# Retention in steps of 64 tokens on quarters of the TensorE array, in a kernel of retention and a Mish feed-forward

## The chip, the core and the metric

The kernel runs on one core of one Trainium2 chip. The metric is the device time of one execution in microseconds; lower is better. Three runs of the kernel before gave 208.31, 208.77 and 209.69 us, a median of 208.77. One execution was taken with the hardware profiler: it took 209.11 us, and the span from its first to its last instruction is 207.2 us.

## The reference: what is computed

Retention over 4 sequences of 768 tokens with 8 heads of 64, then a feed-forward layer with the weights w_in (512 x 2048) and w_out (2048 x 512), in fp32 at its ends:

```
gamma = 1.0 - 2.0 ** (-5.0 - np.arange(H))
for t in range(S):
    state = gamma * state + k[t] (outer) v[t]      # 64x64 for each head
    y[t] = scale * q[t] @ state
x = y, as 3072 rows of 512
h = x @ w_in
g = h * np.tanh(np.log1p(np.exp(h)))               # Mish
out = g @ w_out
```

## The kernel before

**Chunks and blocks.** The 3072 tokens are 24 chunks of 128 (C, six in a sequence). Block 0 has the first four chunks, blocks 1 to 10 two each. (In all texts here blocks and chunks are counted from 0; the sixth block is block 5.) Each block goes through retention, a first product with w_in and Mish, and a second product with w_out.

**Retention of a chunk** is computed chunkwise, heads in four pairs. The decay within a chunk is in the scaled q and v that `casts` makes on POOL (L211 on), so no decay stands in the matmuls:
- `scores` (L258): at = k q, eight matmuls that contract over the 64 rows of a head, so a head takes half of the array's rows; two heads of a pair take the two halves.
- `mask` (L269): DVE multiplies at by a triangle and writes am in fp16.
- `outer` (L280): u_ps = k v for a pair of heads in one 128 x 128 matmul, four of them. Half of each result belongs to no head.
- `state` (L290): DVE adds the last state and multiplies by gcm, which holds the decay of 128 tokens and is zero off the heads' own blocks. The state is 128 x 512.
- `past` (L303): y_ps = state q, four matmuls over the whole array.
- `present` (L310): y_ps += v am, eight matmuls that write half of the columns each.
- ACT casts y_ps to xt (L392), the input of the first product.

`scores_two`, `outer_two` and `y_two` (L364 to L393) do this for the two chunks of a block, with PSUM tiles of the pool atps (two tiles of two banks each). The pool mmps has four tiles of one bank.

**The feed-forward of a block.** `g1` (L397) makes 128 x 512 of h_ps per step: eight matmuls of 256 columns for a block of two chunks, and Mish on ACT. Blocks 1 and 2 do the second product straight (`g2_mm`, L416, 128 x 512). From block 3 on (SEVEN = 3) `seven` (L478) does the second product as a 2 x 2 product of blocks with seven multiplications: DVE makes sums of g (sums_a, sums_b, sums_c: L464 to L476), TensorE does seven products of eight matmuls into the tiles pb, pe and px, ACT takes copies of a tile between them (`snap`, L502), and DVE writes the results (`done`, L507). A `snap` of pe must be over before pe is added to again.

**Order of the work.** The order is written out by hand. Each engine takes its instructions in the order in which the program names them. The loop at L657 runs the steps u of a block; `plan_of` (L638) says behind which step the work for the next block stands: outer_two behind u=0, scores_two behind u=3, and y_two (as a hook of `seven`, L525) after the third of the seven products. In blocks 1 and 2 scores, outer and y stand behind steps 7 to 14. `next_chunk` (L632) casts, transposes (q and k of a chunk by DMA on SP's queue) and issues loads that are three chunks ahead. Stores stand on SP's queue too (L170).

Of the kernel before, what the change touches and what calls it, by code (L numbers as in the profile page):

```python
# [16 lines left out]
def kernel(  # L17
# [45 lines left out]
    gp = ctx.enter_context(tc.tile_pool(name="rn_g", bufs=2))  # L63
    op = ctx.enter_context(tc.tile_pool(name="rn_o", bufs=5))
    mmps = ctx.enter_context(
        tc.tile_pool(name="rn_mmps", bufs=4, space=bass.MemoryType.PSUM))
    atps = ctx.enter_context(
        tc.tile_pool(name="rn_atps", bufs=2, space=bass.MemoryType.PSUM))

# [6 lines left out]
    ident = cpool.tile([P, P], FP16, name="ident")  # L76
    tri = cpool.tile([P, C], FP32, name="tri")
    gcm = cpool.tile([P, HP, P], FP32, name="gcm")
    warm = cpool.tile([P, 1], FP32, name="warm")
    nc.gpsimd.memset(ident, 0.0)  # L80
    nc.gpsimd.affine_select(  # L81
# [4 lines left out]
        out=tri, in_=tri, compare_op=ALU.is_gt, fill=1.0, base=0,  # L86
        pattern=[[-1, C]], channel_multiplier=1)

    tri_first = cpool.tile([P, CPB, C // CPB], FP32, name="tri_first")
    nc.gpsimd.memset(tri_first, 0.0)  # L90
    nc.gpsimd.affine_select(
        out=tri_first, in_=tri_first, compare_op=ALU.is_gt, fill=1.0, base=0,
        pattern=[[-1, CPB], [-CPB, C // CPB]], channel_multiplier=1)
    nc.vector.memset(warm, 0.0)
    nc.scalar.activation(warm, warm, AF.Mish)
    nc.vector.memset(gcm, 0.0)
# [5 lines left out]
    wout_ap = moe_w_out.rearrange("(fb p) c -> p fb c", p=P)  # L102

    qfirst_t = cpool.tile([P, HP, CPB, P], FP16, name="qfirst_t")
    loaded, cast, qkts, ats, ams, states, us, ys = {}, {}, {}, {}, {}, {}, {}, {}
    xts, gts, wins, wouts, wtmps = {}, {}, {}, {}, {}
    gtiles, tmats, gsums = {}, [], []
    SEVEN = 3
# [102 lines left out]
    def casts(g):  # L211
        qf, kf, vf = loaded.pop(g)
        qk16 = castp.tile([P, 2, H, D], FP16, name="qk16")
        q16, k16 = qk16[:, 0], qk16[:, 1]
        v16 = castp.tile([P, H, D], FP16, name="v16")
        if qf is not None:
            nc.gpsimd.tensor_tensor(  # L217
                q16, qf, qs.unsqueeze(2).broadcast_to((P, H, D)), op=ALU.mult)
        if g < CPB + 2:
            nc.scalar.mul(k16, kf, BOOST)  # L220
        else:
            nc.gpsimd.tensor_scalar(k16, kf, BOOST, None, op0=ALU.mult)  # L222
        nc.gpsimd.tensor_tensor(  # L223
            v16, vf, vs.unsqueeze(2).broadcast_to((P, H, D)), op=ALU.mult)
        cast[g] = (q16, k16, v16, qk16)

    def turn_by_dma(g):
        qkt = qktp.tile([P, H, C], FP16, name="qkt", bufs=4)
        nc.sync.dma_start_transpose(qkt, cast[g][3].rearrange("p a h d -> p (a h d)"))
        qkts[g] = (qkt[:, :HP], qkt[:, HP:])  # L230

# [15 lines left out]
    def turn(g):  # L247
        q16, k16 = cast[g][:2]
        t_ps = atps.tile([P, H, C], FP16, name="t_ps", tag="at")
        for i in range(HP):  # L250
            nc.tensor.transpose(t_ps[:, i], q16[:, 2 * i:2 * i + 2], ident)
        for i in range(HP):
            nc.tensor.transpose(t_ps[:, HP + i], k16[:, 2 * i:2 * i + 2], ident)
        qkt = qktp.tile([P, H, C], FP16, name="qkt", bufs=4)
        nc.vector.tensor_copy(qkt, t_ps)
        qkts[g] = (qkt[:, :HP], qkt[:, HP:])

# [61 lines left out]
    def last_of_batch(g):  # L319
        return g % NCH == NCH - 1  # L320
# [2 lines left out]

    def outer_one(g):
        if not last_of_batch(g):
            outer(g, mmps.tile([P, HP, P], FP32, name="u_ps", tag="mm"), states.get(g - 1))

    def xt_first(g, pairs=slice(None)):
        n = C // CPB
# [31 lines left out]

    def scores_two(blk):  # L364
        a = first[blk]
        scores(a)
        scores(a + 1)
        mask(a)
        mask(a + 1)

    def outer_two(blk):
        a = first[blk]
        u_ps = atps.tile([P, 2, HP, P], FP32, name="u_ps", tag="at")
        for j in range(2):
            if not last_of_batch(a + j):
                outer(a + j, u_ps[:, j])
        for j in range(2):
            if not last_of_batch(a + j):
                state(a + j)

    def y_two(blk):
        a = first[blk]
        y_ps = atps.tile([P, HP, 2, C], FP32, name="y_ps", tag="at")
        inter = a % NCH > 0
        if inter:
            past(a, lambda i: y_ps[:, i, 0], lambda i: i % 2 == 0)
        past(a + 1, lambda i: y_ps[:, i, 1], lambda i: not inter and i % 2 == 0)
        for j in range(2):
            present(a + j, lambda i: y_ps[:, i, j], lambda i: False)
        xt = xtp.tile([P, HP, TB], FP16, name="xt")  # L390
        xts[blk] = xt
        nc.scalar.copy(  # L392
            xt[:, :, :2 * C], y_ps.rearrange("p i j c -> p i (j c)"))  # L393

    def g1(blk, u):  # L397
        nt = BLOCKS[blk] * C
        per = TB // nt
        h_ps = mmps.tile([P, per, nt], FP32, name="h_ps", tag="mm")  # L400
        for j in range(per):
            s, f = divmod(u * per + j, FPS)
            for bp in range(NBP):
                nc.tensor.matmul(  # L404
                    h_ps[:, j], wins[s][f // 2][:, bp, f % 2 * P:(f % 2 + 1) * P], xts[blk][:, bp, :nt],
                    start=(bp == 0), stop=(bp == NBP - 1))
        room = NFB * TB // (2 * nt)
        at0, lies = divmod(u * per, room)
        if lies == 0:
            gtiles[blk, at0] = gp.tile([P, room, nt], FP16, name="g", tag="g", bufs=4)  # L410
        gt = gtiles[blk, at0][:, lies:lies + per]
        nc.scalar.activation(gt, h_ps, AF.Mish, scale=inv_boost3)  # L412
        for j in range(per):
            gts[blk, u * per + j] = gt[:, j]
# [62 lines left out]

    def seven(blk, hooks, last):  # L478
        n, hf = NFB // 2, d_model // 2
        ps = [mmps.tile([P, hf], FP32, name="o_ps", tag="mm") for _ in range(3)]  # L480
        pb, pe, px = ps
        osb = [op.tile([P, d_model], FP32, name="osb", tag="osb") for _ in range(2)]

        def a(i, j):
# [5 lines left out]
        def s(i):  # L490
            return lambda f: gsums[blk % 2][:, i - 1, f]
# [30 lines left out]
        mm(px, s(2), t(2))  # L522
        u2 = snap(px)
        sums_c(blk)
        for fn, *args in hooks:  # L525
            fn(*args)
        mm(pe, s(1), t(1), True)
        m5 = snap(pe)
        mm(px, s(3), t(3))
        done(1, 1, px, m5)  # L530
# [31 lines left out]
    def first_block():  # L562
# [18 lines left out]
        for g in range(CPB):  # L581
            last = g == CPB - 1
            if not last:
                cast_to(g + 2)
            scores(g)
            mask(g, 2 if last else 1)
            if g > 0:
                y_one(g - 1)
            if not last:
                at_tile(g + 1)  # L590
                outer_one(g)
                spin(g + 1, 2 if g else 8)
                turn_k(g + 1)
                state(g)
                spin(g + 1, (12, 10, 8)[g])
        y_one_in_halves(CPB - 1)
        outer_one(CPB - 1)
        cast_win(0)
# [16 lines left out]
        for u in range(2 * NFB):  # L615
            if u < NFB:
                g1(0, u)
            elif u < 2 * NFB - 2:
                w = u - NFB
                for t in range(CPB):  # L620
                    if w == 0:
                        o_tiles[t] = mmps.tile([P, d_model], FP32, name="o_ps", tag="mm")
                    g2_mm(o_tiles[t], 0, t, w)
            else:
                for t in range(CPB // 2) if u % 2 == 0 else range(CPB // 2, CPB):
                    for w in range(NFB - 2, NFB):
                        g2_mm(o_tiles[t], 0, t, w)
                    g2_out(o_tiles[t], 0, t, 1)
            for fn, *args in plan.get(u + 1, ()):
                fn(*args)  # L630

    def next_chunk(g):  # L632
        if g < NCK:
            cast_to(g + 1)
            turn_by_dma(g)
            load_to(g + 3)

    def plan_of(blk):  # L638
        a = first[blk] + 4
        if blk >= SEVEN:  # L640
            plan = {1: [(cast_to, a + 1), (next_chunk, a)],
                    7: [(cast_to, a + 2), (next_chunk, a + 1)]}
            if blk + 1 < len(BLOCKS):
                plan[0] = [(outer_two, blk + 1)]
                plan[3] = [(scores_two, blk + 1)]
            return plan
        early, then_seven = blk == 1, blk + 1 == SEVEN
        plan = {1: [(cast_to, a + 1)],
                (1 if early else 2 if then_seven else 4): [(cast_to, a + 1), (next_chunk, a)],
                (5 if early else 8): [(cast_to, a + 2), (next_chunk, a + 1)]}  # L650
        plan[10 if early else 7] = [(scores_two, blk + 1)]
        plan[12 if early else 10] = [(outer_two, blk + 1)]
        plan[14 if early else 13] = [(y_two, blk + 1)]
        return plan

    first_block()
    for blk in range(1, len(BLOCKS)):  # L657
# [20 lines left out]
            if extra:  # L678
                extra.pop(0)()
        if blk >= SEVEN:  # L680
            seven(blk, [] if last else [(y_two, blk + 1)], last)
    store_due(2 * NFB)


# [28 lines left out]
```

## Time and profile before

| What | us |
|---|---|
| median of three runs | 208.77 |
| the profiled execution | 209.11 |
| its span | 207.2 |
| TensorE (PE) busy | 199.7 |
| VectorE (DVE) busy | 118.6 |
| ScalarE (ACT) busy | 86.6 |
| GpSimd (POOL) busy | 77.1 |
| matmuls of 256 columns for h_ps (L404), 640 of them, each | 0.273 |
| the masks of blocks 1 to 10 (L275), each | 1.22 |
| a cast of y_ps to xt (L392), each | 1.01 |

PE is the matmuls, PEld the loads of the stationary operand, which lie beside them. A matmul's record is longer than the step to the next one, since matmuls are pipelined: starts of L404 are 0.109 us apart though each record is 0.273. Steps between starts therefore tell what a matmul costs in a row of them, and records do not. A line such as L404 is a line of the kernel as printed above. In the chain of waits each piece is followed back from the last instruction to what released it.

### The profile page before, as it was taken

How to read it: one execution, taken by the hardware profiler on the slowest of the kernel's cores; microseconds unless marked ns; L12 is line 12 of the kernel's file. 1: busy time of each engine (PE TensorE's matmuls, PEld its weight loads, DVE VectorE, ACT ScalarE, POOL GpSimd, SP SyncE). 2: the span in 40 equal slices, each digit the busy share in tenths (PEclk: the TensorE clock that was granted, in tenths of full speed). 3: DMA queues.
4: the chain of work that ended last, by engine and by line, in shares of the span. 5: the costliest groups of instructions: out<-in, count | busy, mean ns of one | idle time of the engine just before them, and what ended most of it. 6: DMA issues, size and time to landing. Idle time of an engine off the chain costs nothing.

```text
span 207.2 us, 4555 instructions
## 1 busy us (share of the span) xinstructions
PE 199.7 (96%) x1909; PEld 150.4 (73%) x1909; DVE 118.6 (57%) x184; ACT 86.6 (42%) x146; POOL 77.1 (37%) x72
## 2 busy tenths in 40 slices
PE   7798999999999999999999999999999999999993
PEld 2454444445865775788888888888888888898883
DVE  2696544257209779475666686474574773573062
ACT  2243665043540650464354363453453453453640
POOL 3242000326966186577547358267066000000000
PEclk9999999999999999999999999999999999999999
DMA  5999999998899999999999799696897910200202
GB/s 179 235 223 341 381 387 349 233 294 180 159 235 279 207 197 230 193 232 207 242 237 179 114 245 153 164 244 101 189 203 118 180 26 5 101 0 23 82 27 77
DMA packets 99989, 38.59 MB, mean 186 GB/s; under 512 B 90497, under 2 KB 94081, under 8 KB 99969
## 3 DMA queue, kind: packets, MB, share of 16 engines
q1 hardware_dynamic: 96704, 37.50, 85.6%
q10 hardware_dynamic: 3264, 0.81, 2.4%
q8 instruction: 15, 0.25, 0.5%
q14 instruction: 6, 0.04, 0.1%
HBM read 27.29 MB, written 6.29 MB: 162 GB/s over the span
## 4 chain that ended last, share of the span: by engine, by line
PE 80%; DMA 9%; SPq 7%; ACT 1%; DVE 1%; issue 1%; ACTq 0%
PE h_ps L404 38%; PE o_ps L498 24%; PE o_ps L418 9%; DMA wi<-in_moe_w_in_dram 5%; SPq L122 5%; DMA kf<-in_k_dram 3%; PE y_ps L315 3%; PE at L265 3%; PE y_ps L305 2%; PE u_ps L283 2%; SPq L140 1%; ACT xt L392 1%; SPq L181 0%; DVE win L157 0%; ACT qk L220 0%
## 5 line engine op out<-in xcount | busy, mean ns | idle before, releaser
L404 PE MATMUL h_ps<-xt,win 128*128 128x256 f16 (+1 forms) x704 | 88.0, 282 | 1.1 <-DVE win L157 0.7
L412 ACT ACTIVATE g<-h_ps 128x512 f16<-128x512 f32 x96 | 57.3, 597 | 58.3 <-PE h_ps L404 58.3
L404 PEld LDWEIGHTS <-win 128*128 128x128 f16 x704 | 67.9, 98 | 17.6 <-DVE win L157 1.6
L217 POOL TENSOR_TENSOR qk<-qf,qvs 128x512 f16<-128x512 f32 x20 | 22.3, 1117 | 61.4 <-DMA qf<-in_q_dram 54.0
L275 DVE TENSOR_TENSOR am<-at,tri 128x1024 f16<-128x1024 f32 x20 | 23.7, 1220 | 18.1 <-PE at L265 18.0
L223 POOL TENSOR_TENSOR v<-vf,qvs 128x512 f16<-128x512 f32 x24 | 25.7, 1072 | 17.4 <-DMA vf<-in_v_dram 11.4
L418 PE MATMUL o_ps<-wout,g 128*128 128x512 f16 x128 | 30.1, 380 | 0.0
L222 POOL TENSOR_SCALAR qk<-kf 128x512 f16<-128x512 f32 x18 | 27.5, 1528 | 4.1 <-DMA kf<-in_k_dram 2.9
L498 PEld LDWEIGHTS <-gsum 128*128 128x128 f16 x256 | 24.5, 98 | 3.4
L498 PE MATMUL o_ps<-tmat,gsum 128*128 128x256 f16 x192 | 23.5, 273 | 0.0
L418 PEld LDWEIGHTS <-g 128*128 128x128 f16 x128 | 11.7, 98 | 13.0 <-issue 0.3
L512 DVE TENSOR_TENSOR osb<-o_ps,snap 128x256 f32<-128x256 f32 x24 | 10.1, 422 | 19.0 <-ACT snap L504 15.9
L498 PEld LDWEIGHTS <-g 128*128 128x128 f16 x192 | 18.8, 98 | 2.2
L392 ACT CAST xt<-y_ps 128x1024 f16<-128x1024 f32 x10 | 10.1, 1012 | 21.6 <-PE y_ps L315 21.6
L467 DVE TENSOR_TENSOR gsum<-g 128x512 f16<-128x512 f16 x16 | 7.8, 490 | 13.3 <-ACT g L412 13.2
L498 PE MATMUL o_ps<-wout,g 128*128 128x256 f16 x128 | 15.3, 273 | 0.0
L504 ACT COPY snap<-o_ps 128x256 f32<-128x256 f32 x24 | 8.9, 373 | 13.7 <-PE o_ps L498 13.7
L298 DVE TENSOR_TENSOR su<-u_ps,st 128x512 f32<-128x512 f32 x13 | 9.0, 692 | 5.0 <-PE u_ps L283 4.8
L243 PE MATMUL at<-ident 128*128 128x512 f16 (+1 forms) x34 | 9.8, 411 | 1.3 <-POOL ident L81 1.3
L299 DVE TENSOR_TENSOR st<-su,gcm 128x512 f16<-128x512 f32 x13 | 9.1, 703 | 0.4
L220 ACT ACTIVATE qk<-kf 128x512 f16<-128x512 f32 x6 | 3.8, 630 | 12.8 <-DMA kf<-in_k_dram 12.8
L157 DVE CAST win<-wi 128x1024 f16<-128x1024 f32 x8 | 5.4, 692 | 6.1 <-DMA wi<-in_moe_w_in_dram 6.1
(59 smaller groups left out, 146.2 us busy)
## 6 DMA issues: line engine op xcount, KB each, us to landing
kf<-in_k_dram SPq DMA_DIRECT2D x23, 256.0 KB, 4.7
vf<-in_v_dram SPq DMA_DIRECT2D x23, 256.0 KB, 5.0
out_dram<-osb SPq DMA_DIRECT2D x22, 256.0 KB, 4.4
qf<-in_q_dram SPq DMA_DIRECT2D x19, 256.0 KB, 4.0
wt<-in_moe_w_out_dram SPq DMA_DIRECT2D x3, 1024.0 KB, 10.1
wi<-in_moe_w_in_dram SPq DMA_DIRECT2D x4, 512.0 KB, 7.6
wi<-in_moe_w_in_dram SPq DMA_DIRECT2D x2, 1024.0 KB, 11.1
qfirst<-in_q_dram SPq DMA_DIRECT2D x2, 512.0 KB, 5.0
```

Source lines behind the costliest of these rows:

```text
L122: queue.dma_start(loaded[g][n], (q, k, v)[n][b, :, c * C:(c + 1) * C].rearrange("h p d -> p h d"))
L217: nc.gpsimd.tensor_tensor(q16, qf, qs.unsqueeze(2).broadcast_to((P, H, D)), op=ALU.mult)
L222: nc.gpsimd.tensor_scalar(k16, kf, BOOST, None, op0=ALU.mult)
L223: nc.gpsimd.tensor_tensor(v16, vf, vs.unsqueeze(2).broadcast_to((P, H, D)), op=ALU.mult)
L243: nc.tensor.matmul(ats[g][:, 0, :m], ident, ident.unsqueeze(1).broadcast_to((P, m, P)), start=True, stop=True)
L275: nc.vector.tensor_tensor(am[:, :, i:i + n], at[:, :, i:i + n], keep.unsqueeze(1).unsqueeze(1).broadcast_to((P, 2, n, C)), op=ALU.mult)
L392: nc.scalar.copy(xt[:, :, :2 * C], y_ps.rearrange("p i j c -> p i (j c)"))
L404: nc.tensor.matmul(h_ps[:, j], wins[s][f // 2][:, bp, f % 2 * P:(f % 2 + 1) * P], xts[blk][:, bp, :nt], start=(bp == 0), stop=(bp == NBP - 1))
L412: nc.scalar.activation(gt, h_ps, AF.Mish, scale=inv_boost3)
L418: nc.tensor.matmul(o_ps, gts[blk, fb][:, t * P:(t + 1) * P], wouts[s][:, f, cols], start=(fb == 0), stop=(fb == NFB - 1))
L498: nc.tensor.matmul(o_ps, x(f), w(f), start=first and f == 0, stop=f == n - 1, skip_group_check=True)
L512: nc.vector.tensor_tensor(dst, o_ps, plus, op=ALU.add)
```

## The change

From block 2 on retention runs in steps of 64 tokens, so that every matmul of it is 64 x 64 with 64 columns and sits on a quarter of the array. The first half and the second half of a chunk have states of their own: `mid_of` makes the state at a chunk's middle, `state_of` that at its end, both compact (128 x 256, a head pair's two states below each other, no empty halves). The scores between the halves of a chunk are no longer computed; the state in the middle carries them. Only the diagonal 64 x 64 blocks of at are made and masked (`tri_half`).

`ready` gives outer products and scores as pairs of matmuls, `same` for the quarters on the array's diagonal and otherwise for the others; `run` takes from several streams in turn. `past_of` is on the diagonal quarters alone. Between `past_of` and `present_of`, which write the same banks from other row halves, DVE reads one element of each bank (`seen`), and present waits for that.

- For blocks 2 to 5 `get_ready` does outer and scores in one place of the block before (behind u=10 in block 1, u=7 in block 2, u=2 in blocks 3 and 4).
- For y of blocks 5 to 9 `retain` stands in `seven` of the block before with past of that block, outer and scores of the block after it, and present, all in one place; the states and masks of these follow behind u=0 of the next block (`settle`).
- For blocks 4 and 10 `seven` has past after the third product and `finish` (present and the casts) after the fourth, before its snap.
- In blocks 1 and 2 past stands behind u=13 and present behind u=14.
- The cast of y_ps to xt is in two instructions, one for each bank.
- PSUM: mmps has three tiles, and a new pool pxps has one, which takes px of `seven`, and h_ps of some steps. There are three buffers of g, not four; six of qkt; seven of v16.
- From chunk 10 on loads are issued one chunk further ahead, and chunk 15 asks for two at once.

```diff
+    def score(at, j, g, i, hh, s):
+        qt, kt = qkts[g]
+        nc.tensor.matmul(
+            at[half(s), hh, j, i], kt[half(hh), i, half(s)], qt[half(hh), i, half(s)],
+            start=True, stop=True)
+
+    def outer_half(u, j, g, i, hh, s):
+        _, k16, v16, _ = cast[g]
+        if s == 0 or not last_of_batch(g):
+            nc.tensor.matmul(
+                u[half(hh), s, j, i], k16[half(s), 2 * i + hh], v16[half(s), 2 * i + hh],
+                start=True, stop=True)
...
+    def ready(blk, same):
+        at, u = held[blk]
+        for fn, t in ((outer_half, u), (score, at)):
+            for j in range(2):
+                for i in range(HP):
+                    yield [
+                        lambda fn=fn, t=t, j=j, i=i, hh=hh: fn(
+                            t, j, first[blk] + j, i, hh, hh if same else 1 - hh)
+                        for hh in range(2)]
...
+    def settle(blk):
+        a = first[blk]
+        at, u = held.pop(blk)
+        for j in range(2):
+            us[a + j] = u[:, :, j]
+        mid_of(a)
+        state_of(a)
+        mid_of(a + 1)
+        am = tpp.tile([P, 2, 2, HP, D], FP16, name="am")
+        nc.vector.tensor_tensor(
+            am.rearrange("p a j i c -> p (a j i) c"), at.rearrange("p a j i c -> p (a j i) c"),
+            tri_half.unsqueeze(1).broadcast_to((P, 4 * HP, D)), op=ALU.mult)
+        for j in range(2):
+            ams[a + j] = am[:, :, j]
+        state_of(a + 1)
+
+    def get_ready(blk):
+        hold(blk)
+        run(ready(blk, True), ready(blk, False))
+        settle(blk)
...
+    def retain(blk, later=None, spread=False):
+        if spread:
+            ys[blk] = [
+                mmps.tile([P, 2, HP, D], FP32, name="y_ps", tag="mm") for _ in range(2)]
+        else:
+            y = pair_tile(atps, "y_ps", "at")
+            ys[blk] = [y[:, s] for s in range(2)]
+        if later is None:
+            run(past_of(blk))
+        else:
+            hold(later)
+            run(past_of(blk), ready(later, False))
+        for s in range(2):
+            nc.vector.tensor_copy(seen, ys[blk][s][:, 1, 0, :1])
+        if later is not None:
+            run(ready(later, True))
+            finish(blk)
+
+    def finish(blk):
+        present_of(blk)
+        xt = xtp.tile([P, HP, TB], FP16, name="xt")
+        xts[blk] = xt
+        dst = xt[:, :, :2 * C].rearrange("p i (j s c) -> p j i s c", j=2, s=2)
+        for s in range(2):
+            nc.scalar.copy(dst[:, :, :, s], ys[blk][s])
...
         sums_c(blk)
-        for fn, *args in hooks:
+        for fn, *args in hooks[0]:
             fn(*args)
+        pe = mmps.tile([P, hf], FP32, name="o_ps", tag="mm")
         mm(pe, s(1), t(1), True)
+        for fn, *args in hooks[1]:
+            fn(*args)
         m5 = snap(pe)
...
+        if blk > SEVEN + 1:
+            return {0: [(settle, blk + 1)] if blk + 1 < len(BLOCKS) else [],
+                    1: [(next_chunk, a + 1)]}
         if blk >= SEVEN:
+            plan = {2: [(get_ready, blk + 1)]}
+            if blk == SEVEN:
+                plan[0] = [(cast_to, a + 1), (next_chunk, a)]
+                plan[4] = [(cast_to, a + 2), (next_chunk, a + 1)]
+            else:
+                plan[1] = [(next_chunk, a + 1)]
+            return plan
...
+        plan[10 if early else 7] = [(get_ready, blk + 1)]
+        plan[13] = [(retain, blk + 1)]
+        plan[14] = [(finish, blk + 1)]
...
+            hooks = [[], []]
+            if not last:
+                later = blk + 2 if SEVEN < blk < len(BLOCKS) - 2 else None
+                hooks = [[(retain, blk + 1, later, True), (next_chunk, first[blk] + 6)],
+                         [(finish, blk + 1)] if later is None else []]
+            seven(blk, hooks, last)
```

## The prediction, made before the result was known

> **What bounds the kernel now.** I read the page's head and slices first (who is busy, at which clock), then the chain of waits as shares, then that chain in order of time, and last the timeline of one spot and the starts of its single matmuls.
>
> ```profile
> span 207.2 us, 4555 instructions
> PE 199.7 (96%) x1909; PEld 150.4 (73%) x1909; DVE 118.6 (57%) x184; ACT 86.6 (42%) x146; POOL 77.1 (37%) x72
> PE   7798999999999999999999999999999999999993
> DVE  2696544257209779475666686474574773573062
> PEclk9999999999999999999999999999999999999999
> PE 80%; DMA 9%; SPq 7%; ACT 1%; DVE 1%; issue 1%; ACTq 0%
> ```
>
> TensorE is busy in all but the first slices, at the full granted clock, and 80% of the chain is its own. The DMA and SPq shares belong to the start: the last of them is a K load that lands at 41.5 us. Nothing that I say below moves that landing, so all counts after it. Next, the chain in time for one block from the sixth on (columns: start, us, what):
>
> ```profile
> 99.92 0.87 PE h_ps L404 x8
> 100.79 0.45 PE u_ps L283 x8
> 101.24 2.62 PE h_ps L404 x24
> 103.86 0.55 PE at L265 x16
> 104.41 3.60 PE h_ps L404 x32
> 108.01 2.62 PE o_ps L498 x24
> 110.63 0.22 PE y_ps L305 x4
> 110.86 0.57 PE y_ps L315 x16
> 111.42 3.60 PE o_ps L498 x32
> ```
>
> There is no wait in it: retention's matmuls (u_ps, at, y_ps) stand in line with the two products. So what the edit does to retention's TensorE time, and any wait that it brings, is all that counts. Now the spot of y_ps in the timeline, every engine:
>
> ```profile
> 110.30 0.42 DVE L512 TENSOR_TENSOR osb<-o_ps,snap 128x256 f32<-128x256 f32 x1
> 110.47 0.39 PE L305 MATMUL y_ps<-qkt,st 128*128 128x128 f16 x4
> 110.64 1.20 DVE L476 TENSOR_TENSOR gsum<-g,gsum 128x1024 f16<-128x1024 f16 x1
> 110.67 0.37 ACT L504 COPY snap<-o_ps 128x256 f32<-128x256 f32 x1 [1.37 <-PE o_ps L498]
> 110.79 0.64 PE L315 MATMUL y_ps<-am,v 128*64 128x128 f16 x16
> 111.47 1.01 ACT L392 CAST xt<-y_ps 128x1024 f16<-128x1024 f32 x1 [0.42 <-PE y_ps L315]
> 112.44 0.37 ACT L504 COPY snap<-o_ps 128x256 f32<-128x256 f32 x1
> ```
>
> Three things to see. Sixteen L315 matmuls of 0.22 us fit in 0.64: they run in pairs. In the trace's single starts the two of a pair (the two column halves) are 3 ns apart and pairs 56 ns apart, just as whole-array matmuls of 128 columns (L283, L305) are 56 apart; L265's row halves pair likewise. Second, a change of array shape costs: the last whole matmul to the first of L265 is 205 ns where 109 is the step, and 148 ns pass on the way out where 53 is the step. Third, DVE's gsum L476 ends 1.37 us after y_ps begins, and ACT does the y_ps cast before the second snap.
>
> **The change part by part.**
> *Retention on TensorE, removed* (blocks 2 to 10, counted from 0). Per block: scores 8 x 56 ns + 0.21 of shape changes (205-109, 11 of a first weight load, 148-53, 10 of a first step) = 0.66; present 8 x 56 + 0.225 = 0.673; outer and past 4 x 56 = 0.223 per chunk, of which 15 each exist (18 chunks less 3 at an end of a sequence). 9 x (0.66 + 0.673) + 30 x 0.223 = 18.7 us.
>
> *Added.* 1104 matmuls of 64x64x64 for 408, by the built order of instructions. They stand as 216 steps of up to four on different quarters (get_ready, past with the later block's off-diagonal half, present) and 140 steps of two (past alone, the later block's diagonal half). Price of a step: 256 columns take 109.2 ns, 128 take 55.8, so 64 extrapolate to 29, if all quarters run at once as halves do. Low end 26.7 (columns alone, -0.85 us in all); high end 28 ns for each matmul, the mean of the pairs seen. I take 29, since in the pairs the second costs nothing: 356 x 29 ns = 10.3 us. A first weight load of 64 columns delays by 24 ns in L315, so a visit costs 0.225; the visits fall from 18 (scores, present) to 17 (three for each of blocks 1 to 3, two in block 4, one in 5 to 8, two in 9): 3.8 us. Sum 14.15, saving 4.55.
>
> [...]
>
> *Waits added.*
> (a) Block 1: y_ps takes over the PSUM buffer of at, so past waits for the mask. get_ready starts at 61.9 where the scores do; its outer products are done at about 62.45; then DVE does mid, suh, sth, mid (0.42 each, as L512) and one mask (1.22), with 0.035 between: 65.6 with the way back. PE is there at 61.87 + 0.70 + 12 x 0.216 = 65.16. 0.47 us.
> (b) xt: two casts of 0.574 (L341's size) instead of one of 1.01, and in block 2 four L418 matmuls behind present, not eight. From present's last start: casts begin at 0.26, end at 1.36, seen at 1.47; four L418 end at 1.03. 0.44 in block 2; in block 1, which waits 0.35 now, 0.09 more.
> (c) Blocks 3 and 9: finish stands between pe's first product and its snap, so ACT does both casts (to 1.36) and then the snap (0.37) before pe may be added to; L504 then ends at 1.71, 1.82 with the way back, and PE is there at 1.04 after eight matmuls. 2 x 0.78 = 1.57. In blocks 4 to 8 sixteen matmuls lie between: no wait.
> (d) Blocks 4 to 8: present waits for two tiny DVE copies ("seen") of y_ps. Each is worth 0.16 (L424 and L510 differ by 1.02 ns an element, which leaves that). Past ends 0.80 after y_ps begins; PE, with the later block's diagonal half as cover, is at present at 0.12 + 32 x 0.029 = 1.05; both copies are back 0.4 after they can start: 0.2 short. But they queue behind L476, which ends 1.37, 1.48, 0.84, 0.83, 0.63 after y_ps begins in these five blocks; the two late ones have it at 1.20 us instead of 0.68, with POOL's casts beside it. Casts come a chunk earlier now, so I charge the first of them (1.37 + 0.4 - 1.05 = 0.7) and 0.2 for the others: 1.5. Bounds: 0 (copies in L476's shadow and past shorter) and 5 x 0.75 = 3.75.
> Behind a waiting PE stand the rest of the seven products; behind a late xt the next block.
>
> *At no cost, with their cover.* DVE gets less: masks 2 x 1.22 to 1.22, states 2 x 1.4 to four or six of 0.42; if settle were late, present would be too, but it has from u=0 to the end of seven, 10 us, for 3.7. mmps of 3 plus pxps of 1 are the four banks of now; a bank of h_ps comes back two products of 0.87 later, and ACT needs 0.6 of that (L412). gch, tri_half: POOL waits for the q load at 39 anyway. SP: each step of next_chunk (a transpose, 4.4 us to landing, and three loads of 4 to 5) moves past the stores, and loads run a chunk ahead; chunks 14 and 15, first used by ready in block 4 at 110, have their transposes in block 3's seven and behind u=1 of block 4, at about 96 and 101, so they land by about 106. Were that cover gone, PE would wait in ready at most the landing, 4.4. A block takes one of the g buffers (block 0 two), so with three of them one is taken again two blocks later: free.
>
> *Sum.* Profiled execution 209.11 (span 207.2 and 1.9 around it), 0.34 above the median of 208.77. -4.55 + 0.47 + 0.53 + 1.57 + 1.5 = -0.48: 208.6 for it, 208.3 for the median.
>
> **The rivals.**
> R1, slower: only two quarters run at once. Then a step of four is 58 ns: +6.3 us, while (d) shrinks to 0.26 in one block. -4.55 + 6.3 + 2.57 + 0.26 = +4.5: 213.3. It decides from 31 ns a step on: 0.48 / 216 is 2 ns. For it: no row shows more than two tiles at once. Against: halves by rows and by columns both cost nothing.
> R2, slower: the queue cannot hand out matmuls faster than the 28 ns each that pairs average. 1104 x 28 ns + 3.8 = 34.7, 16 more than now; (d) vanishes: +18.6, 227.4. For it: 28 ns a matmul is all that any row shows on average. Against: pairs leave 3 ns apart, and PE had over 30 instructions in hand where its sequencer's waits show it. [...]
> R3, faster: the small waits are covered, (a) and (d) nothing. -4.55 + 2.1 = -2.45: 206.3. For it: DVE is lighter and POOL earlier; against: (d) has 0.2 even without L476.
> R4, about even: L476 is late in all five blocks. +2.25 on the sum: 210.5. For it: two of five are late now.
> That the edit does not run four quarters at all is R1.
>
> **How the numbers follow.** About 1% (2.1 us) is what a measurement here can tell from no change. The forecast, 206.7 to 209.4, gets 0.45; R3 0.17, R4 0.12, R1 0.17, R2 0.09. Faster by over 1% (below 206.7): R3 nearly whole and a little of the forecast, 0.18. Slower by over 1% (above 210.9): R1, R2 and half of R4, 0.32. Within: 0.50. The range leaves out R2 and the low end of R3, and reaches from 205.9 to 213.5.
>
> **What would show it.** Steps: starts of u_ps, at and y_ps in the 64x64 form, 29 ns from four to four (58: R1; 28 ns throughout: R2), and the time from the first to the last of a visit in block 5, 40 steps in 1.2 us plus the wait. (c): PE idle about 0.8 before the product with wout behind present in blocks 3 and 9, released by ACT's snap. (d): PE idle before present, released by DVE, 0.2 to 0.7. (a), (b): idle before y_ps at 65 and before h_ps in block 3. The forecast is wrong if quarters don't overlap, or if a wait appears in ready for a transpose or a cast.

## The result, and the profile after

The changed kernel takes 210.94 us (median of 20 runs, 209.82 to 215.49) where the kernel before takes 209.01 beside it: a ratio of 1.0093, 95% interval 1.0067 to 1.0118. It is slower by just under 1%, where the forecast was 208.3. The profiled execution took 211.49 us. Its page, the lines that answer to those shown of before:

```profile
span 209.7 us, 6000 instructions
PE 198.5 (95%) x2605; PEld 148.1 (71%) x2605; DVE 112.7 (54%) x214; ACT 86.8 (41%) x155; POOL 76.8 (37%) x82
...
PE   7798999999998999898998998999999999999993
...
DVE  2796444277017985355287558445645843662062
...
PEclk9999999999999999999999999999999999999999
...
PE 59%; SPq 12%; DMA 12%; POOL 5%; DVE 4%; issue 3%; ACT 2%; POOLq 0%; DVEq 0%
```

The clock is full as before. TensorE's row now has eights in the middle, and its share of the chain has fallen from 80% to 59%: POOL, DVE, ACT and the transposes have come onto the path. The view of TensorE's waits names them (columns: who waited for whom, us in total, times, longest; it counts idle time behind a matmul's record, which is longer than the step, 0.195 us for the 64x64 form and 0.273 for 256 columns, so a late start counts only in part here and the starts of single matmuls give larger numbers below; gsum L601 is the second of the sums of g, called s2 here, and the product that waits for it reads it):

```profile
PE o_ps L631 <- ACT snap L637: 1.1, 2, 0.6
PE y_ps L473 <- DVE seen L513: 1.0, 2, 0.5
PE at L394 <- DMA qkt<-qk: 0.8, 2, 0.5
PE o_ps L631 <- DVE gsum L601: 0.7, 2, 0.5
PE h_ps L537 <- ACT xt L524: 0.5, 2, 0.3
...
PE y_ps L473 <- DVE am L459: 0.2, 1, 0.2
```

Of these six only the fifth was there before, in part. The chain in order of time shows where block 4 stands still; before, this stretch had nothing but TensorE's own pieces:

```profile
109.29 0.61 ACT g L545
109.90 0.02 issue
109.92 0.97 DVE gsum L600
110.89 0.02 issue
110.92 0.13 DVE gsum L601
...
112.57 1.33 DVE gsum L609
113.90 0.08 DVE seen L513
...
114.28 0.44 PE y_ps L473 x30
```

To set the two traces side by side I take the window from block 1's first h_ps to the last matmul, 151.52 us before (52.29 to 203.81) and 154.62 after (51.66 to 206.28): +3.10. (Block 1 starts between 51.5 and 52.7 in the profiles of this study whatever is edited, and this execution lies 0.55 above its median, so the medians differ by less, 1.93.) For each gap between two matmuls I take the usual step off. That gives two sums. Waits: 0.35 before, 6.46 after, so +6.1. Retention's own TensorE time without waits: 18.51 in 27 visits before, 15.5 in 17 visits after, so -3.0. The forecast had +4.07 and -4.55. Both terms were off, each by about 1.5 to 2 us, and in the same direction.

By block the picture is clearer (from first h_ps to first h_ps, us):

| block | 1 | 2 | 3 | 4 | 5 | 6 | 7 | 8 | 9 |
|---|---|---|---|---|---|---|---|---|---|
| before | 16.25 | 16.11 | 15.11 | 15.10 | 15.33 | 15.10 | 15.10 | 15.33 | 15.10 |
| after | 16.95 | 16.30 | 16.42 | 16.83 | 16.28 | 14.71 | 14.54 | 14.66 | 14.94 |

Blocks 6 to 8, which do retention in one place and wait for nothing, gain 0.4 to 0.7 each. Blocks 1 to 5 lose all of that and more.

**Single starts.** In get_ready and in the mixed visits (past, the later block's outer products and scores, and present in one place) the four matmuls of a step start 3 to 4 ns apart and the next four begin some 22 ns later: a step of four is 32 ns. After about 45 matmuls of a get_ready visit the starts become even, 8 to 9 ns each, 33.5 ns for four. Steps of two matmuls (past alone) take 32 ns as well. A step of four thus costs what a step of two does, so I take it that all four quarters run at once; R1's 58 ns and R2's 28 ns throughout are refuted. The step is 32 to 34 ns, not 29. The groups by line and shape agree in that nothing waits inside most of it (last column):

```profile
L394 PE MATMUL at<-qkt 64*64 64x64 f16 x288 | 7.0, 195 | 0.8 <-DMA qkt<-qk 0.8
L401 PE MATMUL u_ps<-v,qk 64*64 64x64 f16 x264 | 6.1, 195 | 0.0
```

### The profile page after: what moved, and what is told of

Read it like the earlier page. It is cut to its first block, busy times and chain, and to the rows that moved or that the text cites. A ratio compares the mean times of both kernels' runs of the same rounds, so it can differ in the third digit from the quotient of the medians.

```text
span 209.7 us, 6000 instructions
## 1 busy us (share of the span) xinstructions
PE 198.5 (95%) x2605; PEld 148.1 (71%) x2605; DVE 112.7 (54%) x214; ACT 86.8 (41%) x155; POOL 76.8 (37%) x82
## 4 chain that ended last, share of the span: by engine, by line
PE 59%; SPq 12%; DMA 12%; POOL 5%; DVE 4%; issue 3%; ACT 2%; POOLq 0%; DVEq 0%
PE h_ps L537 31%; PE o_ps L631 21%; SPq L128 8%; DMA kf<-in_k_dram 5%; DMA wi<-in_moe_w_in_dram 3%; PE o_ps L551 3%; PE y_ps L473 3%; POOL qk L228 3%; SPq L235 2%; DMA qf<-in_q_dram 2%; DMA qkt<-qk 2%; POOL qk L223 1%; POOL v L229 1%; DVE gsum L609 1%; DVE gsum L600 1%
## 5 line engine op out<-in xcount | busy, mean ns | idle before, releaser
L537 PE MATMUL h_ps<-xt,win 128*128 128x256 f16 (+1 forms) x704 | 86.0, 282 | 1.3 <-ACT xt L524 0.5
L537 PEld LDWEIGHTS <-win 128*128 128x128 f16 x704 | 68.6, 98 | 17.5 <-issue 2.0
L223 POOL TENSOR_TENSOR qk<-qf,qvs 128x512 f16<-128x512 f32 x20 | 21.2, 1060 | 51.1 <-DMA qf<-in_q_dram 35.0
L229 POOL TENSOR_TENSOR v<-vf,qvs 128x512 f16<-128x512 f32 x24 | 25.1, 1044 | 18.5 <-DMA vf<-in_v_dram 16.0
L631 PE MATMUL o_ps<-tmat,gsum 128*128 128x256 f16 x192 | 24.2, 273 | 0.7 <-DVE gsum L601 0.7
L600 DVE TENSOR_TENSOR gsum<-g 128x512 f16<-128x512 f16 x16 | 9.1, 567 | 23.2 <-ACT g L545 23.2
L524 ACT CAST xt<-y_ps 128x512 f16<-128x512 f32 x18 | 9.7, 588 | 26.1 <-PE y_ps L473 26.1
L631 PE MATMUL o_ps<-wout,g 128*128 128x256 f16 x128 | 15.3, 273 | 0.0
L459 DVE TENSOR_TENSOR am<-at,tri_half 128x1024 f16<-128x1024 f32 x9 | 10.9, 1215 | 0.0
L631 PE MATMUL o_ps<-wout,gsum 128*128 128x256 f16 x64 | 8.3, 273 | 1.1 <-ACT snap L637 1.1
L438 DVE TENSOR_TENSOR mid<-u_ps,sth 128x256 f16<-128x256 f32 x15 | 6.3, 422 | 3.7 <-PE u_ps L401 3.4
```

The costliest lines, as they stand in the source:

```text
L223: nc.gpsimd.tensor_tensor(q16, qf, qs.unsqueeze(2).broadcast_to((P, H, D)), op=ALU.mult)
L229: nc.gpsimd.tensor_tensor(v16, vf, vs.unsqueeze(2).broadcast_to((P, H, D)), op=ALU.mult)
L459: nc.vector.tensor_tensor(am.rearrange("p a j i c -> p (a j i) c"), at.rearrange("p a j i c -> p (a j i) c"), tri_half.unsqueeze(1).broadc ...
L537: nc.tensor.matmul(h_ps[:, j], wins[s][f // 2][:, bp, f % 2 * P:(f % 2 + 1) * P], xts[blk][:, bp, :nt], start=(bp == 0), stop=(bp == NBP - 1))
L600: nc.vector.tensor_tensor(s1, a21, a22, op=ALU.add)
L631: nc.tensor.matmul(o_ps, x(f), w(f), start=first and f == 0, stop=f == n - 1, skip_group_check=True)
```

## The experiments

Theory A: the gain on the array is real but small, and the loss is a handful of waits with separate causes, each of which can be taken away. Rivals: the side parts of the edit cost by themselves (C); DVE is held by POOL's casts, so that waits only move (D, later L); a wait taken away is replaced by the next.

**e1, the snap ahead of the casts.** In `seven`:

```diff
         mm(pe, s(1), t(1), True)
+        m5 = snap(pe)
         for fn, *args in hooks[1]:
             fn(*args)
-        m5 = snap(pe)
```

> The changed kernel with one move: in the second product of blocks 3 and 9 ScalarE takes the copy m5 of pe before present and its two casts, not after them. Theory A (each added wait is lost time by itself): the two waits of TensorE for that copy, 0.75 and 0.63 us in the profile after, go, and the time falls by about 1.4 us, from a ratio of 1.009 to about 1.003. Theory B (the waits are slack of something else, and what is saved in one place is waited for in the next): xt is later instead or the next product waits for a sum, and the time stays within 0.3 us of the changed kernel's.

Measured: 210.63 us, ratio 1.0058 (1.003 to 1.0086). Both waits for the snap, 0.75 and 0.63 in the trace of after, are gone; the waits for transposes and for seen are left:

```profile
PE y_ps L473 <- DVE seen L513: 1.0, 3, 0.5
...
PE h_ps L537 <- ACT xt L524: 0.5, 2, 0.3
PE at L394 <- DMA qkt<-qk: 0.5, 2, 0.3
```

Step (c) of the prediction had the right mechanism. The ratio falls by 0.35%, 0.7 us, half of the waits that went and half of what was expected, but the two intervals overlap, so the time alone does not show a gain.

**e2, seen ahead of the sum.** `sums_c(blk)` moves behind hooks[0], so the tiny copies no longer queue behind L609.

> The changed kernel with one move: VectorE does the two one-element copies (seen) before the sum s4 (L609), not after it. Theory A (present waits because the copies stand behind a sum that takes 1.4 us in blocks 4 and 5): the waits before present there, 0.8 and 0.36 us, fall to about 0.2 each, the sum of L609 is late for nobody (its reader is three products away), and the time falls by 0.5 to 0.8 us: ratio about 1.006. Theory B (the round trip TensorE, VectorE, TensorE itself is the wait): the waits stay over 0.5 and the time does not move. Theory C: VectorE now stands waiting for past before it can do s4, and s4 becomes late: a new wait before the product of s4 with wout.

Measured: 211.03, ratio 1.0084 (1.006 to 1.0108), no different from after. The waits for seen in blocks 4 and 5 are gone, but ready's scores in block 5 wait 1.02 for a transpose in their place (0.51 in after), and two products with s2, in blocks 3 and 5, wait 0.31 each:

```profile
PE at L394 <- DMA qkt<-qk: 1.3, 2, 0.9
PE o_ps L631 <- ACT snap L637: 1.0, 2, 0.5
```

TensorE came to these scores 1.07 us sooner after block 1's start than in after, so part of what the waits for seen gave back was waited for again here. One trace does not say how much of the 1.02 is that.

**e3, loads one chunk less ahead, from chunk 15 on only.** `load_to(g + 4)` where after has `g + 5`.

> The changed kernel with loads from chunk 15 on one chunk less far ahead (chunk 15 asks for one more chunk, not two); casts are asked for as before. Theory A (the transposes of q and k are late since they stand behind loads on SP's queue, which waits for the DMAs of eight issues before): the transpose of chunk 17 is issued some 5 us earlier than 125.5, the 0.51 us wait of scores in block 4's second product or block 5's goes, and the casts of k on POOL fall elsewhere, so that the slow sums of blocks 4 and 5 may move too: time down by 0.5 us or more. The wait of 0.59 in block 3 (chunk 11) stays, as nothing before chunk 15 is moved. Theory B (the transposes wait for casts, or the DMA engines are simply full): the transpose stays where it is and the loads that come later make a new wait for a cast.

Measured: 211.65, ratio 1.0093 (1.0064 to 1.0123). Block 5's wait for a transpose is gone, but block 3's, which this edit does not touch, is 1.52 in this execution (0.59 in after). Inconclusive in time; the same wait differs by 0.93 us between these two executions.

**e4, the scores in two matmuls of 32 columns.** The same columns in twice as many matmuls, each with its own weight load:

```diff
-        nc.tensor.matmul(
-            at[half(s), hh, j, i], kt[half(hh), i, half(s)], qt[half(hh), i, half(s)],
-            start=True, stop=True)
+        for c in range(0, D, D // 2):
+            nc.tensor.matmul(
+                at[half(s), hh, j, i, c:c + D // 2], kt[half(hh), i, half(s)],
+                qt[half(hh), i, s * D + c:s * D + c + D // 2], start=True, stop=True)
```

> Measures what a step on the quarters costs: the changed kernel with each scores matmul of 64 columns split into two of 32, each with its own load of the same 64 stationary columns. In the profile after, four matmuls on four quarters step by 34 ns where I had 29. If the step is bound by the 64 moving columns, the scores half of a get_ready visit (8 steps of 34 ns) becomes 16 steps of about 18 and its time hardly moves; if it is bound by the load of 64 stationary columns or by a floor per matmul, it becomes 16 steps of about 33, 0.27 us more per visit; if the queue gives out so many instructions a time (8 in 34 ns), steps of two would also be half as long as steps of four, which the profile after does not show.

Measured: 220.63 (one run). A visit of get_ready has 96 matmuls, not 64, and takes 0.859 us from first to last start, not 0.550. That is 0.31 more, the size expected of a load or a floor, but the starts show another reason than a step of 33. Late in the visit they come 8.4 ns apart one after another, and the 32 added matmuls cost 9.7 ns each. Two 32-column matmuls on one quarter are about 17 ns apart, each with its load of 64 weights. So the weight load, the same beside 17 ns as beside 32, does not set the step of 32. Nor do the 8.4 ns alone, as steps of two also take 32. That leaves the columns, 26.7 ns for 64 by the prediction's line, with about 5 ns beside them; this is inferred, and what the 5 ns are no run shows. Late in a long visit of after the 8.4 ns show again: 33.5 for four matmuls of 64 columns. The whole time says little, since the trace also has a wait of 3.29 for a transpose, one of 2.96 with no releaser shown, and 3.4 us at a granted clock of 0.5 behind the latter.

**e5, the edit without its retention.** The kernel before with the loads further ahead (but not the additional cast from chunk 15 on), the buffers for v and qkt, three banks and one aside, three g buffers and pe taken late; retention as it was.

> The kernel before with all of the edit but the retention itself: loads further ahead, more buffers for v and the turned q and k, three PSUM banks and one aside, three g buffers, pe taken late; retention as it was. Theory A (the loss is made by retention's own waits and by the price of a step): the side parts are free, ratio to before 0.998 to 1.003, and PE's waits from 50 us on stay at about 0.6 us in all. Rival C (the loads ahead and the split of the banks cost by themselves): PE waits for transposes or for h_ps here too, 1 us or more, ratio 1.005 to 1.01.

Measured: 210.24, ratio 1.0054 (1.0031 to 1.0076): half of the loss without a single quarter matmul. From 52.5 us on its waits are before's 0.35 and one new one of 1.68 in block 3, at the scores of chunk 11. The first line of its waits:

```profile
PE at L271 <- DMA qkt<-qk: 1.5, 1, 1.5
```

Rival C holds for the loads ahead: theirs is the only new wait in the trace. Nothing waits for a bank or a g buffer, so that part of "at no cost" stood.

**e8, after with the loads as before.**

```diff
-            if g < 15:
-                load_to(g + 3 if g < 10 else g + 4)
-            else:
-                cast_to(g + 2)
-                load_to(g + 5)
+            load_to(g + 3)
```

> The changed kernel with one edit: loads run three chunks ahead throughout as before, without the additional cast ahead. Theory S (the transposes are late because SP issues more loads ahead of them): the waits of scores for transposes (0.59 in block 3, 0.13 in block 4, 0.51 in block 5) go, transposes of chunks 11 to 17 are issued 2 us or more earlier; 209.7, ratio 1.003 to 1.006. Rival D (the waits of blocks 4 and 5 come from DVE's sums beside POOL's casts, and the loads only move them): ratio 1.007 to 1.011, with the waits for gsum and seen as large as before.

Measured: 210.00, ratio 1.0037 (1.0019 to 1.0056): 0.56%, 1.2 us, back. What it does is seen on SP's queue, after first, then e8 (start, time that SP spent on issuing, what):

```profile
83.75 1.16 SPq L179 DMA_DIRECT2D out_dram<-osb  x1
85.01 1.31 SPq L235 DMA_TRANSPOSE qkt<-qk  x1
86.37 0.80 SPq L128 DMA_DIRECT2D qf<-in_q_dram  x1
```

```profile
79.48 1.36 SPq L179 DMA_DIRECT2D out_dram<-osb  x1
80.94 1.32 SPq L235 DMA_TRANSPOSE qkt<-qk  x1
82.32 1.27 SPq L128 DMA_DIRECT2D qf<-in_q_dram  x1
```

In after SP issues one DMA after another from 77 to 131 us with hardly a gap, 0.4 to 2.7 us each. The transpose of chunk 11 stands behind the additional chunk's three loads (79.26 to 83.64): 85.01 against 80.94, and the scores of chunk 11 want it at 88.1. It did not wait for its casts, which POOL had done by 79.3. No wait for a transpose is left in e8 (1.23 in after). Theory S stands, and D too in its way: the waits for seen did not go but came to four blocks (4 to 7), 0.2 for the second copy in each and 0.1 to 0.55 for the first in three: much as R4 had it, though 1.6 us in all.

**e6, five small moves.** After with e1, e2 and e8 together, get_ready of blocks 3 and 4 one step later, and block 2's retain and finish one step earlier (the last for the xt of block 3).

> The changed kernel with five moves: the snap ahead of the two casts, the seen copies ahead of sums_c, loads three chunks ahead as before, block 3's and 4's get_ready one step later, block 2's retain and finish one step earlier. Theory A: 1.4 (snap) + 0.43 (xt) + 1.2 (transposes) + 0.8 (seen) of the 6.8 us of waits go, 0.23 + 0.55 + 0.42 in block 1 and about 1 for gsum sums stay or shrink: 207, ratio 0.988 to 0.993. Rival D (DVE's sums beside POOL's casts stay slow and only move the wait, as with the seen copies alone): 1.8 go, ratio about 1.000. Rival C (each wait taken away is replaced by the next): ratio above 1.004.

Measured: 207.05, ratio 0.9888 (0.9855 to 0.9922): theory A's range, and faster than both kernels. Waits fall from 6.46 to 2.64, and of those one is new in size, 1.22 in block 4, a product with s2 that waits for DVE:

```profile
PE o_ps L631 <- DVE gsum L601: 1.3, 2, 1.1
...
PE h_ps L537 <- ACT xt L524: 0.3, 1, 0.3
```

**e7, the same moves and no block in one place.** Blocks 4 to 9 do as block 3.

> As e6_five_small_moves, and no block does retention in one place: blocks 4 to 9 do as block 3 (get_ready at the fourth step, past and present around the first product of pe). Theory A: one place saves a visit of about 0.2 us and little else in each of blocks 4 to 8, so this is 1.0 slower than e6 at equal waits, but the later block's scores no longer come a block early and the seen copies have a product as cover, so about 1 us of waits goes: 207 to 208, ratio 0.990 to 0.996, within 0.3% of e6. Rival D (one place itself is the gain): 1.5 us or more slower than e6.

Measured: 209.66, ratio 1.0025 (1.0001 to 1.0049), 2.6 us slower than e6: D's side, and I had expected 1.0. Retention's TensorE time without waits is 17.1 in 27 visits, against 15.3 in e6's 17. With 0.5 more of waits that is the 2.3 by which e7's window is longer. So quarters in visits of their own gain only 1.4 on before's 18.5; one place for two blocks' work gains another 1.8, 0.18 for each visit that it saves.

**e9 to e11, why DVE is late.** In e6's timeline of block 4, settle and the sums of g follow each other on DVE while POOL casts:

```profile
104.60 1.04 POOL L229 TENSOR_TENSOR v<-vf,qvs 128x512 f16<-128x512 f32 x1
106.69 1.04 POOL L223 TENSOR_TENSOR qk<-qf,qvs 128x512 f16<-128x512 f32 x1 [1.05 <-DMA qf<-in_q_dram]
107.82 1.49 POOL L228 TENSOR_SCALAR qk<-kf 128x512 f16<-128x512 f32 x1
109.39 1.04 POOL L229 TENSOR_TENSOR v<-vf,qvs 128x512 f16<-128x512 f32 x1
```

```profile
104.99 0.93 DVE L447 TENSOR_TENSOR sth<-suh,gch 128x256 f16<-128x256 f32 x1
105.95 0.42 DVE L438 TENSOR_TENSOR mid<-u_ps,sth 128x256 f16<-128x256 f32 x1
...
107.88 0.83 DVE L447 TENSOR_TENSOR sth<-suh,gch 128x256 f16<-128x256 f32 x1
108.63 0.41 DVE L600 TENSOR_TENSOR gsum<-g 128x512 f16<-128x512 f16 x1
109.08 0.43 DVE L601 TENSOR_TENSOR gsum<-gsum,g 128x512 f16<-128x512 f16 x1
109.42 1.29 DVE L600 TENSOR_TENSOR gsum<-g 128x512 f16<-128x512 f16 x1
```

The mid, with an input in PSUM, takes its 0.42 here as in after, where all 15 take 0.414 to 0.425; sth (128x256) and gsum (128x512), with both inputs in SBUF, take 0.42 or up to 1.29. The one that starts at 109.42, just after POOL's cast of v, ends 0.28 after that cast. Ten traces of this study (before, after, e1 and e5 to e11) show how often DVE operations with both inputs in SBUF are longer beside the q and v casts: of 111 that started while one ran, 97 were longer by over 50 ns; of 47 that such a cast started behind, none; of 369 with no POOL operation beside them, none. Those 97 ended as if they had begun 0.90 us into the cast of 1.04 or later. Beside the cast of k (1.49 us, TENSOR_SCALAR) it is less regular: only 38 of 113 were longer, and these ended as if they had begun 0.5 to 0.8 us after its start, well ahead of its end. What in the chip makes them longer no trace shows.

e9 moves block 4's get_ready from u=3 to u=1; e10 leaves the order and puts the sum into PSUM; e11 does both:

```diff
-            su = stp.tile([P, HP, D], FP32, name="suh")
-            nc.vector.tensor_tensor(su, u[:, 1], mids[g], op=ALU.add)
+            su = u[:, 1]
+            nc.vector.tensor_tensor(su, su, mids[g], op=ALU.add)
```

> e6_five_small_moves with block 4's get_ready at its second step, not its fourth. In e6 settle's seven DVE operations run from 104.1 to 108.7, right ahead of the sums, and the product of s2 waits 1.22 us for them. Theory Q (the sums are late because settle stands ahead of them in DVE's queue): settle ends two steps, 1.7 us, earlier, the wait falls to 0.3 or less: 0.9 to 1.2 us faster than e6, ratio to before 0.982 to 0.985. Rival L (the sums are late because DVE cannot run an operation with both inputs in SBUF while POOL casts, wherever settle stands): the wait stays at 0.8 or more, ratio 0.987 to 0.990.

> e6_five_small_moves with the sum of mid and the second half of u written back into its place in PSUM, not to SBUF, so that the state's product has one input in PSUM. A test of what slows DVE beside POOL. Theory L (only operations with both inputs in SBUF are held by POOL's): the product of sth never takes over 0.45 us, where in e6 it takes 0.42 to 1.1, settle in block 4 is 0.9 shorter and the wait of the s2 product falls from 1.22 to about 0.4; ratio 0.983 to 0.987. Rival M (any DVE operation that writes 16-bit data is slowed beside POOL): sth still takes up to 1.1 us and the ratio stays at 0.987 to 0.990.

> e9 and e10 together. Theories Q and L both give less than their sum, since it is one wait: no wait for gsum in block 4, what is left is 0.4 in block 6, 0.4 of the xt in block 1 and 0.2 to 0.5 of past and present there: 205.5 to 206, ratio 0.982 to 0.985. If neither holds: 207, 0.988.

Measured: e9 206.49, ratio 0.9866 (0.9846 to 0.9885); e10 206.54, 0.987 (0.9848 to 0.9892); e11 205.71, 0.9846 (0.9828 to 0.9864). In all three the wait for gsum in block 4 is gone. In e10 every one of the 15 products of sth takes 0.424 or 0.425 us. Seven of them started while a POOL operation ran, as the one at 107.19 here; the one at 104.80 started 0.05 ahead of a cast:

```profile
104.85 1.04 POOL L229 TENSOR_TENSOR v<-vf,qvs 128x512 f16<-128x512 f32 x1
106.70 1.04 POOL L223 TENSOR_TENSOR qk<-qf,qvs 128x512 f16<-128x512 f32 x1 [0.81 <-DMA qf<-in_q_dram]
```

```profile
104.33 0.43 DVE L445 TENSOR_TENSOR u_ps<-u_ps,mid 128x256 f32<-128x256 f32 x1
104.80 0.42 DVE L447 TENSOR_TENSOR sth<-u_ps,gch 128x256 f16<-128x256 f32 x1
...
107.19 0.42 DVE L447 TENSOR_TENSOR sth<-u_ps,gch 128x256 f16<-128x256 f32 x1
```

So theory L is shown, and M (any 16-bit result) is out. Q is shown as well, as settle's place alone also clears the wait. Both are shown by the traces: in time each gains about 0.5 us on e6, for e9 less than expected, and the intervals overlap e6's. e11 came as expected. Why e9's median gained less than its wait is not shown. Its profiled execution was its slowest (209.04, 2.5 above the median), and there the scores wait 2.23 for a transpose, which the view has as:

```profile
PE at L394 <- DMA qkt<-qk: 2.1, 1, 2.1
```

e10's profiled execution has such a wait of 0.56, e11's none. e11's page, and the two waits that its view lists behind block 1's start (both in block 1: h_ps for xt, y_ps for am):

```profile
span 204.0 us, 5998 instructions
...
PE 197.5 (97%) x2605; PEld 148.1 (73%) x2605; DVE 111.6 (55%) x214; ACT 87.0 (43%) x155; POOL 80.1 (39%) x82
```

```profile
PE h_ps L537 <- ACT xt L524: 0.3, 1, 0.3
...
PE y_ps L473 <- DVE am L459: 0.2, 1, 0.2
```

Why the scores in block 4 wait for a transpose, 2.23 us in e9's execution and not at all in e11's, stays open: the loads were three chunks ahead in e6, e9, e10 and e11 alike, and no run here took other traffic off the DMA engines at that time.

## Why the prediction was wrong

It forecast a small gain where there was a small loss: inside its range, on the wrong side of no change. In the profiled window the forecast misses by 3.6 us, and three steps that failed make nearly all of it, over a microsecond each: the price of a step on the quarters (29 ns, measured 32, which makes 1.2 us), the transposes said to be covered (1.23 us of waits), and DVE's sums of g, put at nothing (1.05 us of waits). The time lies near R4's 210.5, but not for R4's reason.

*Removed, 18.7.* The trace of before has 18.51. Right.

*Added, 14.15.* Measured 15.5 in after, without waits, and 15.3 in e11. The step that failed is "I take 29, since in the pairs the second costs nothing". That the others cost nothing held; the 29 did not. The line through whole-array matmuls (109.2 and 55.8 ns) leaves 2.4 ns beside the columns, and matmuls of 64 columns on quarters have about 5. With the visits at 3.8 as predicted, (15.3 - 3.8) / 356 is 32.3 ns for a step, and the single starts show 32 to 34. That is 1.2 us, and 2 ns on each step of four was the whole of the forecast gain, as R1's paragraph had said. No rival had it: all quarters at once, but 3 ns more. (R1 and R2 are refuted by the starts, 32 ns a step; R3 by waits that stayed; R4's late L609 came in two blocks. "Over 30 instructions in hand", said against R2, is not what the trace of before has: between a sequencer's wait from 60 us on and the load that it stands ahead of, 1 to 19 matmuls and loads start.) R2's mean of 28 ns for each matmul is in none of these visits: a step of four has 8 ns for each, a step of two 16.

*(a) 0.47.* Past in block 1 waits 0.23. But present, one step on, waits 0.55: its seen copies stand behind an osb copy (L557) and a slowed sth (0.80). I had seen "seen" only in blocks 4 to 8.

*(b) 0.53.* 0.07 in block 1 and 0.43 in block 2: right.

*(c) 1.57.* 0.75 and 0.63: right, and e1 shows the cause.

*(d) 1.5.* 1.18, all in blocks 4 and 5 (0.62 + 0.20 and 0.16 + 0.20): the cause right, the blocks not. In blocks 6 to 8 the copies cost 0.02 at most, not 0.2, and block 5's late L609 (1.41) came instead: that the sums are near is in part luck. Beside it the products with s2 wait 0.41 and 0.64 for L601, which no step had: DVE's sums of g were charged nowhere, though the trace of before showed L476 at 1.20 instead of 0.68 beside POOL's casts, and its L468, after's L601, at up to 1.15 instead of 0.42. I used the first row and did not ask which other operations read twice from SBUF.

*At no cost: SP and the transposes.* This cover failed: "chunks 14 and 15 ... land by about 106". Chunk 15's transpose was issued at 109.27 (105.67 before), because from chunk 10 on an additional chunk's loads, 4.4 us of SP's time, stand ahead of all that follows, and SP had no gap in which to catch up. The same delay hits chunk 11 in block 3, which the prediction did not look at. 1.23 us of waits in after; e8 gives 1.2 back, and e5, with no other new wait, loses 1.1.

*Sum.* Predicted -4.55 + 4.07 = -0.48; measured -3.0 + 6.1 = +3.1 in the profiled window, +1.93 in medians. The waits that no step had are the transposes with 1.23 and the s2 products with 1.05; (a) to (d) came to 3.84, 0.2 less than the 4.07 charged; as (a)'s new wait for seen is among them, that too is partly luck.

## What to carry to other kernels

Here one engine was at 96%, and two thirds of the miss came from the queues beside it. Check for each moved DMA what its queue issues ahead of it, and whether that queue has gaps at all, before calling it covered. The fixed part of a large matmul's step need not hold for a smaller one (2.4 ns beside the columns for 128x128 with 128 and 256, about 5 for 64x64 with 64): where no row has the shape, weigh the gain against an error of a few ns times the number of steps. And a wait that is taken away alone may show only the next one (e2: nothing), while the same move stands in a set that counts (e6: 2% from after).

## What was not expected of the hardware

On quarters of the array four matmuls start 3 to 4 ns apart, but a step of four 64x64x64 matmuls is 32 ns, not the 29 that larger shapes suggest, and late in a get_ready visit each matmul with its weight load takes 8.4 ns. A visit of quarters costs about 0.18 us beside its steps, so that saving visits (e7 against e6: 1.8 us) was worth more than the quarters themselves (1.4). VectorE operations with both inputs in SBUF took up to 1.29 us instead of 0.42 beside POOL's casts (e6), and the product of sth with one input in PSUM did not (15 of 15 in e10, seven of them started beside a POOL operation).
